# Reordering the first phase of a Fourier mixing and MLP kernel, with identity products in TensorE's waits

## The chip, the cores and the metric

The kernel runs on one core of a Trainium2 chip. The metric is the device time of one execution in microseconds (us). The median of eight runs of the kernel before is 1998.47 us (1996.56 to 2000.04).

The engines are named as in the profile: PE is TensorE's matrix product, PEld its weight load, DVE is VectorE, ACT is ScalarE, POOL is GpSimd and SP is SyncE, which here only issues transfers. The engines run side by side, and each takes its own instructions in the order in which the program issues them.

## What is computed

A real input of 8 x 3008 x 256 goes through a two-dimensional Fourier transform of which the real part is kept, and its rows then through an MLP with squared ReLU:

```python
def _attn_ref(x) -> np.ndarray:          # x: (8, 3008, 256)
    X = np.fft.fft(x, axis=1)
    X = np.fft.fft(X, axis=2)
    return X.real.astype(np.float32)

def _moe_ref(x, w_in, w_out) -> np.ndarray:   # w_in: (256, 2048), w_out: (2048, 256)
    h = x @ w_in
    r = np.maximum(h, 0.0)
    g = r * r
    return (g @ w_out).astype(np.float32)
```

The weights come as 64-bit floating point numbers and are converted to 32 bits on the chip. All products are in 32 bits; in the profile each one is two instructions.

## The kernel before

**Staging.** The transform along the 256 columns is not done on the data: it is multiplied into `w_in`, which gives the tables `G1`, `G2` and `gE`. The transform along the 3008 rows of a batch is a product of folded rows with tables of cosines and sines, and gives `Pt`, `Qt` and `Et` (the cosine part, the sine part, and one single column). The main loop then goes over 8 batches, 6 blocks of at most 251 frequencies and NJ = 8 parts of the 2048 hidden columns, 384 steps in all.

**One step of the loop.** `front` (L402) makes four products, for each of two halves one of `G1` with `Pt` (L412) and one of `G2` with `Qt` (L413), into PSUM tiles `ph`, and VectorE joins them with `Et` and `gE` into `g` (L415, L417, L418). `combine` (L425) lets ScalarE take ReLU and square (L427, L428). `back` (L443) multiplies `g` with `wout` two steps later (LAG = 2), into the PSUM tiles mA to mD. In the first block of the first batch (steps 0 to 7) it uses a plain form (L452) that needs only mA and mB; later steps use the form of L465. During batch b the rows of batch b + 1 are folded and transformed between the pieces of `front`.

**The first phase.** The first batch has nothing to hide behind. SP issues the loads of the first weight, the seven tiles of x and the cosine and sine tables, in this order. Then the following pieces are issued, in an order written out by hand (L568 to L595):

- `for_p(t)`: the three VectorE pieces of the fold that make `wP` of tile t (L297, L307, L308, L317). `for_q(t)`: the three that make `wQ` (L301, L312, L323). P and E are made of all seven `wP`, Q of all seven `wQ`.
- thirty groups, five for each of six transforms: P (0 to 4 and 5 to 9, even and odd frequencies), E (10 to 14, 15 to 19), Q (20 to 24, 25 to 29). In each five, the first is `even_n` (four products on TensorE from tiles 0 to 3, and a copy `da` by ScalarE, L357), the second and third are `join_4` and `join_2` (VectorE), the fourth is `odd_n` (three products from tiles 4 to 6), and the fifth `join_1` writes the result (L362 and L364 or L366). All products are at L349. Their PSUM tiles are two buffers, `psd`.
- the weights, in the order win 0, win 1, wout 0, win 2, wout 1, win 3 and so on. To begin one (`convert`, L187) issues its loads on SP, two VectorE passes (L208, L213) and three ScalarE passes (L210, L211, L215). Its `finish` is three VectorE passes (L218, L220, L221). For a `win` there are also its `products` (L232): `G1` and `G2` (two products each, L236, copied by ScalarE at L237) and `gE` (L242, L244). `next_weight` (L546) begins the next weight and then finishes the current one. The raw data has four buffers: three are shared with the tiles of x (tiles 4 to 6), one is a buffer of its own.

**Order within the loop.** In step i the program issues `front` and `combine`, then `back` of step i - 2, then the `products` collected by the step before, and then up to two calls of `next_weight`.

The clock of TensorE in the profile (PEclk) is the share that the throttle granted; 1.00 is full speed. Before its first change in a trace it is shown as 1.00; durations tell more there.

Of the kernel before, what the change touches and what calls it, by code (L numbers as in the profile page):

```python
# [8 lines left out]
F32 = mybir.dt.float32  # L9
# [4 lines left out]
P = 128  # L14
# [63 lines left out]
def kernel(  # L78
# [12 lines left out]
    nc = tc.nc  # L91
    B, NROW, _, D = x.shape
# [6 lines left out]
    NJ = NFC // 2  # L99
    CH = 256  # L100
# [22 lines left out]
    psm = ctx.enter_context(tc.tile_pool(name="psm", bufs=1, space=PSUM))  # L123
# [7 lines left out]
    def load_x(b, t):  # L131
        _, r0, step, rows = TILES[t]

        while rows % 15 and rows % 16 and r0 + step * rows < NROW:
            rows += 1

        pool, tag = (gp, "g") if b == 0 and t < NT - NX else (xp, "x")
        xt[b, t] = pool.tile([P, 4, D], F32, name="xt", tag=tag)
        nc.sync.dma_start(out=xt[b, t][0:rows], in_=x[b, r0:r0 + step * (rows - 1) + 1:step])
# [8 lines left out]
    ident = const.tile([P, P], F32, name="ident")  # L148
# [4 lines left out]
    def load_table(tab, src, engine):  # L153

        for t, (c, r0, step, rows) in enumerate(TILES):
            for i, (s0, count) in enumerate(row_tiles(S)):
                mine = [r for r in range(count) if (s0 + r - r0) % step == 0 and 0 <= (s0 + r - r0) // step < rows]
                if mine:
                    o, m = (s0 + mine[0] - r0) // step, len(mine)
                    while m % 15 and m % 16 and o + m < P and mine[0] + step * m < P:  # L160
                        m += 1
                    nk = NC[0][c]
                    engine.dma_start(out=tab[o:o + m, :, PLACE[t]:PLACE[t] + nk],
                                     in_=src[mine[0]:mine[0] + step * (m - 1) + 1:step, :, i, 0:nk])
# [4 lines left out]
    nc.vector.memset(ramp[:, 1:2], 255.0 * 2.0 ** 23)  # L169
    for dst, src in ((cosd, cos_d), (sind, sin_d), (altd, alt_d)):  # L170
        nc.scalar.dma_start(out=dst, in_=src.rearrange("(c p) m -> p c m", p=P))


    def pair_in(j):
# [77 lines left out]
    def sum_wout(j):  # L252

        b11, b12, b21, b22 = (wout[:, j, h, c] for c in range(2) for h in range(2))
        t2, t3, t4 = (wsum[:, i, j] for i in range(3))
        tt(out=t3, in0=b22, in1=b12, op=ALU.subtract)
        tt(out=b12, in0=b12, in1=b11, op=ALU.subtract)
        tt(out=t2, in0=b22, in1=b12, op=ALU.subtract)
        tt(out=t4, in0=t2, in1=b21, op=ALU.subtract)
# [9 lines left out]
    def load_column(t):  # L269

        _, r0, step, rows = TILES[t]
        xe[t] = const.tile([P, 4, NE], F32, name=f"xe{t}")
        for i in range(4):
            nc.sync.dma_start(out=xe[t][0:rows, i], in_=x[1:B, r0:r0 + step * (rows - 1) + 1:step, i, H].rearrange("b r -> r b"))
# [127 lines left out]
    def front(b, k0, n, j, between):  # L402

        pt, qt, et = PQE[b]
        ks = slice(k0, k0 + n)
        g = gp.tile([P, 2, 2, CK], F32, name="g", tag="g")
        for h in range(2):
            fc = j + NJ * h
            fs = slice(fc * P, (fc + 1) * P)
            ps = psh.tile([P, 2, CH], F32, name="ph", tag="h")  # L410
            hP, hQ = ps[:, 0, 0:n], ps[:, 1, 0:n]
            nc.tensor.matmul(hP, G1[:, fs], pt[:, ks], start=True, stop=True)  # L412
            nc.tensor.matmul(hQ, G2[:, fs], qt[:, ks], start=True, stop=True)  # L413
            t = hp.tile([P, CK], F32, name="he", tag="he")[:, 0:n]
            nc.vector.scalar_tensor_tensor(out=t, in0=et[:, ks], scalar=gE[:, fc:fc + 1], in1=hP,  # L415
                                           op0=ALU.mult, op1=ALU.add)
            tt(out=g[:, h, 0, 0:n], in0=t, in1=hQ, op=ALU.add)  # L417
            tt(out=g[:, h, 1, 0:n][:, ::-1], in0=t, in1=hQ, op=ALU.subtract)  # L418
            between()
        return g  # L420
# [17 lines left out]
        gt(out=s4, in0=g12, in1=s2, op=ALU.subtract)  # L438
        return s

    acc = {}

    def back(n, j, g, s, final):  # L443

        if j == 0:
            for nm in ("mA", "mB", "mC", "mD"):
                acc[nm] = psm.tile([P, 2, CH], F32, name=nm, tag=nm)
        if s is None:
            for c in range(2):
                for h in range(2):  # L450
                    for side, nm in enumerate(("mA", "mB")):
                        nc.tensor.matmul(acc[nm][:, h, 0:n], wout[:, j, h, c], g[:, c, side, 0:n],  # L452
                                         start=j == c == h == 0, stop=j == NJ - 1 and c == 1, skip_group_check=True)
            return
        products = [("mA", 0, wout[:, j, 0, 0], g[:, 0, 0]),
                    ("mA", 1, wout[:, j, 0, 1], g[:, 1, 0]),
                    ("mB", 0, wsum[:, 2, j], g[:, 1, 1]),
                    ("mB", 1, wout[:, j, 1, 0], s[:, 0]),
                    ("mC", 0, wsum[:, 0, j], s[:, 1]),
                    ("mC", 1, wsum[:, 1, j], s[:, 2]),  # L460
                    ("mD", 0, wout[:, j, 1, 1], s[:, 3])]
        if final and j == NJ - 1:
            products = products[0:2] + products[4:7] + products[2:4]
        for nm, i, w, v in products:
            nc.tensor.matmul(acc[nm][:, i, 0:n], w, v[:, 0:n], start=j == 0 and i == 0, stop=j == NJ - 1,  # L465
                             skip_group_check=True)
# [66 lines left out]
    def ahead(b):  # L533
        ops = [piece for t in range(NT) for piece in fold(b, t)] + dft_ops(b)
        if b == 1:
            ops += [(0.6, lambda t=t: fold_column(t)) for t in range(NT)] + dft_ops(None)
        return ops + [(0.0, lambda: load_e(b))] if b else ops
# [8 lines left out]
    def next_weight():  # L546

        nonlocal begun
        (finish, products), begun = begun, weights.pop(0)() if weights else None
        finish()  # L550
        return products
# [4 lines left out]
    def for_p(t):  # L556
        for i in (0, 2, 4):
            pieces[t][i]()

    def for_q(t):  # L560
        for i in (1, 3, 5):
            pieces[t][i]()

    def groups_at(*which):
        for i in which:
            groups[i]()

    begun = weights.pop(0)()  # L568
    for t in range(NT):
# [1 line left out]
    load_table(cosT, cos_s, nc.sync)  # L571
    load_table(sinT, sin_s, nc.sync)
    start()
    for_p(0)
    finish, products = begun
    finish()
    products()
    for t in range(1, 4):
        for_p(t)
    groups_at(0, 5)  # L580
    for_p(4)
    groups_at(1, 2)
    for_p(5)
    groups_at(6, 7)
    for_p(6)
    groups_at(3)
    for n, t in enumerate((4, 5, 6, 0, 1, 2, 3)):
        for_q(t)
        groups_at(*((4, 8, 9), (10,), (11, 12), (13, 14, 15), (16, 17), (18,), (19,))[n])
    groups_at(20, 25)  # L590
    begun = weights.pop(0)()
    groups_at(21, 22, 23)
    products = next_weight()
    groups_at(26, 27, 28, 24, 29)
    products = [products]  # L595
    LAG = 2
    BLOCKS = [(k0, min(CK, NKT - k0)) for k0 in range(0, NKT, CK)]
    steps = [(b, k0, n, j) for b in range(B) for k0, n in BLOCKS for j in range(NJ)]
# [15 lines left out]
    for i in range(len(steps) + LAG + 4):  # L614
        if i < len(steps):
            b, k0, n, j = steps[i]
            if i == NJ:
                for t in range(NX):
                    load_x(1, t)
            if NJ <= i < NJ + NT:  # L620
                load_column(i - NJ)
            if i % per == 0:
                assert not side
                side = ahead(b + 1) if b + 1 < B else []
                spent, pace = 0.0, sum(t for t, _ in side) / (2 * (per - (0 if i else 2 * NJ)) - 6)
            g = front(b, k0, n, j, between)
            if i < NJ:
                s = combine(n, g, True)
            elif i < 2 * NJ:
                sum_wout(j)  # L630
        while finished and finished[0][0] <= i:
            store(*finished.pop(0)[1:])
        if i >= LAG and flight:
            at, g_, s_ = flight.pop(0)
            final = at[:3] == (B - 1, *BLOCKS[-1])
            back(at[2], at[3], g_, s_, final)
            if at[3] == NJ - 1:
                c_ = gather(at[2], s_ is None, final)
                finished += [(i + 2 + s, *at[:3], s, c_, final) for s in range(2)]
        for f in products:  # L640
            f()
        products = [next_weight() for _ in range(2 if i + 2 < NJ else 1 if i < NJ else 0)]
        if i < len(steps):
            flight.append(((b, k0, n, j), g, s if i < NJ else combine(n, g, False)))

# [62 lines left out]
```

## Time and profile before

| | |
|---|---|
| median of 8 runs | 1998.47 us |
| profiled execution | 1999.46 us |
| its span | 1997.7 us |
| mean granted TensorE clock | 0.993 |
| busy PE / PEld | 1964.2 (98%) / 1706.0 (85%) us |
| busy DVE / ACT / POOL | 1390.6 (70%) / 896.4 (45%) / 1159.0 (58%) us |
| first product of `win` 0 on TensorE | 12.24 us |
| first product of `front`, step 0 | 54.93 us |
| first product of `front`, step 8, after which no weight is left to convert | 120.42 us |

The span runs from the first to the last recorded instruction of the one profiled execution; some 1.8 us of the execution lie around it. Busy time is the sum over the recorded instructions of an engine. A busy TensorE is not TensorE at its peak, since the records of products overlap and become longer where the clock is at half. In the timelines, a bracket at the end of a line gives the idle time of the engine just ahead of the instruction and who ended it.

### The profile page before, as it was taken

What the parts mean: (1) busy time and instruction counts of PE and PEld (TensorE: products, weight loads), DVE (VectorE), ACT (ScalarE), POOL (GpSimd) and SP (SyncE); (2) the same over time, 40 slices, a digit from 0 to 9 for tenths busy, and PEclk for the clock granted to TensorE, in tenths of its full rate; (3) what the DMA queues carried; (4) which work ended last, traced back from release to release, by engine and by line L of the source; (5) the groups of instructions that cost most, each with busy time, mean ns of one, the idle gap of its engine ahead of it and who ended that gap; (6) DMA issues with size and microseconds to landing.
All of it is one profiled execution on the core that took longest, in us unless ns stands there. A gap on an engine that the chain in (4) does not pass through costs nothing.

```text
span 1997.7 us, 27284 instructions
## 1 busy us (share of the span) xinstructions
PE 1964.2 (98%) x9104; PEld 1706.0 (85%) x9104; DVE 1390.6 (70%) x3492; ACT 896.4 (45%) x973; POOL 1159.0 (58%) x1695
## 2 busy tenths in 40 slices
PE   6899999999999999999999999999999999999998
PEld 4788888888888888888888888888888888888887
DVE  7889866776567765787558875677657776555554
ACT  1654434444444444444444444444444454445443
POOL 0026655666566755676556665666656665566664
PEclk8899999999999999999999999999999999999999
DMA  6332101210021111111011110111001100100100
GB/s 183 102 52 49 37 11 32 52 27 22 11 52 32 27 28 30 27 39 40 11 27 37 39 30 11 31 43 37 22 11 45 39 11 16 31 11 11 22 11 21
DMA packets 144687, 68.49 MB, mean 34 GB/s; under 512 B 128440, under 2 KB 135547, under 8 KB 144546
## 3 DMA queue, kind: packets, MB, share of 16 engines
q1 hardware_dynamic: 143470, 66.24, 14.3%
q8 instruction: 71, 1.16, 0.2%
q10 hardware_dynamic: 1076, 0.52, 0.1%
q14 instruction: 70, 0.57, 0.1%
HBM read 42.03 MB, written 24.68 MB: 33 GB/s over the span
## 4 chain that ended last, share of the span: by engine, by line
PE 94%; DVE 3%; ACT 1%; DMA 1%; issue 0%; SPq 0%; DVEq 0%; ACTq 0%
PE ph L412 16%; PE ph L413 16%; PE mA L465 16%; PE mC L465 16%; PE mB L465 16%; PE mD L465 8%; PE pd L349 5%; DMA xt<-in_x_dram 1%; DVE he L415 0%; PE mA L452 0%; PE mB L452 0%; DVE g L418 0%; PE pg L236 0%; DVE fd L301 0%; ACT g L427 0%
## 5 line engine op out<-in xcount | busy, mean ns | idle before, releaser
L427 ACT ACTIVATE g<-g 128x1004 f32<-128x1004 f32 (+1 forms) x384 | 399.5, 1040 | 895.4 <-DVE g L418 483.8
L415 DVE SCALAR_TENSOR_TENSOR he<-Et,gE,ph 128x251 f32<-128x251 f32 (+1 forms) x768 | 361.6, 471 | 476.1 <-PE ph L413 474.5
L435 POOL TENSOR_TENSOR s<-g 128x251 f32<-128x251 f32 (+1 forms) x376 | 248.6, 661 | 745.1 <-ACT g L428 672.3
L412 PE MATMUL ph<-Pt,G 128*128 128x251 f32 (+1 forms) x1536 | 454.3, 377 | 3.5 <-ACT G L237 2.5
L413 PE MATMUL ph<-Qt,G 127*128 127x251 f32 (+1 forms) x1536 | 452.2, 375 | 0.2 <-DVE Qt L362 0.2
L428 ACT ACTIVATE g<-g 128x1004 f32<-128x1004 f32 (+1 forms) x384 | 399.2, 1040 | 12.1
L465 PE MATMUL mC<-s,wsum 128*128 128x251 f32 (+1 forms) x1504 | 381.3, 374 | 0.0
L465 PE MATMUL mA<-g,wout 128*128 128x251 f32 (+1 forms) x1504 | 380.9, 375 | 0.0
L417 DVE TENSOR_TENSOR g<-he,ph 128x251 f32<-128x251 f32 (+1 forms) x768 | 320.4, 417 | 55.6 <-POOL s L437 0.5
L412 PEld LDWEIGHTS ph<-Pt,G 128*128 128x128 f32 x1536 | 287.7, 189 | 47.6 <-DVE g L418 4.0
L413 PEld LDWEIGHTS ph<-Qt,G 127*128 127x128 f32 x1536 | 291.7, 190 | 36.6 <-DVE Qt L362 0.6
L465 PEld LDWEIGHTS mA<-g,wout 128*128 128x128 f32 x1504 | 282.5, 189 | 41.7 <-issue 2.9
L465 PEld LDWEIGHTS mC<-s,wsum 128*128 128x128 f32 x1504 | 285.5, 190 | 34.5
L418 DVE TENSOR_TENSOR g<-he,ph 128x251 f32<-128x251 f32 (+1 forms) x768 | 314.0, 409 | 0.0
L436 POOL TENSOR_TENSOR s<-s,g 128x251 f32<-128x251 f32 (+1 forms) x376 | 281.7, 749 | 29.4
L437 POOL TENSOR_TENSOR s<-g 128x251 f32<-128x251 f32 (+1 forms) x376 | 291.8, 776 | 0.0
L438 POOL TENSOR_TENSOR s<-g,s 128x251 f32<-128x251 f32 (+1 forms) x376 | 246.2, 655 | 0.0
L465 PE MATMUL mB<-g,wsum 128*128 128x251 f32 (+1 forms) x752 | 220.4, 374 | 0.0
L465 PE MATMUL mD<-s,wout 128*128 128x251 f32 (+1 forms) x752 | 220.3, 374 | 0.0
L465 PE MATMUL mB<-s,wout 128*128 128x251 f32 (+1 forms) x752 | 219.9, 374 | 0.0
L465 PEld LDWEIGHTS mB<-g,wsum 128*128 128x128 f32 x752 | 142.6, 190 | 17.4
L465 PEld LDWEIGHTS mD<-s,wout 128*128 128x128 f32 x752 | 141.9, 189 | 17.7
(85 smaller groups left out, 1273.3 us busy)
## 6 DMA issues: line engine op xcount, KB each, us to landing
out_dram<-os SPq DMA_DIRECT2D x376, 56.0 KB
xt<-in_x_dram SPq DMA_DIRECT2D x24, 512.0 KB
xt<-in_x_dram SPq DMA_DIRECT2D x16, 384.0 KB
Et<-e_dram SPq DMA_DIRECT2D x7, 752.5 KB
out_dram<-os SPq DMA_DIRECT2D x288, 6.8 KB
raw<-in_moe_w_in_dram SPq DMA_DIRECT2D x16, 256.0 KB
raw<-in_moe_w_out_dram SPq DMA_DIRECT2D x16, 256.0 KB
xt<-in_x_dram SPq DMA_DIRECT2D x8, 480.0 KB
```

The costliest lines, as they stand in the source:

```text
L412: nc.tensor.matmul(hP, G1[:, fs], pt[:, ks], start=True, stop=True)
L413: nc.tensor.matmul(hQ, G2[:, fs], qt[:, ks], start=True, stop=True)
L415: nc.vector.scalar_tensor_tensor(out=t, in0=et[:, ks], scalar=gE[:, fc:fc + 1], in1=hP, op0=ALU.mult, op1=ALU.add)
L417: tt(out=g[:, h, 0, 0:n], in0=t, in1=hQ, op=ALU.add)
L418: tt(out=g[:, h, 1, 0:n][:, ::-1], in0=t, in1=hQ, op=ALU.subtract)
L427: act(v, v, AF.Relu)
L428: act(v, v, AF.Square)
L435: gt(out=s1, in0=g21, in1=g22, op=ALU.add)
L436: gt(out=s2, in0=s1, in1=g11, op=ALU.subtract)
L437: gt(out=s3, in0=g11, in1=g21, op=ALU.subtract)
L438: gt(out=s4, in0=g12, in1=s2, op=ALU.subtract)
L465: nc.tensor.matmul(acc[nm][:, i, 0:n], w, v[:, 0:n], start=j == 0 and i == 0, stop=j == NJ - 1, skip_group_check=True)
```

## The change

It has four parts, all of them in the first phase and the first steps of the loop.

1. A helper `awake(n)` issues n products of the identity with itself (128 x 128, 32 bits) into the second half of the PSUM tile mD, which the plain steps do not use. The tile is now allocated at the start and taken over by the first `back`.
2. `awake(24)` ahead of the first weight's products, `awake(8)` behind them, `awake(4)` behind each of the twelve `even_n` and `odd_n`, and `awake(8)` in step 1 of the loop, behind `front` and ahead of the products of win 2: 88 products in all.
3. The Q folds, which stood in one row behind the P transforms, are spread: those of tiles 0 and 1 stand ahead of the first `join_4`, those of 4, 5 and 6 between the P and E groups, those of 2 and 3 between the E groups.
4. Weights begin sooner. Win 1 begins behind group 13 instead of behind 25, and is finished (with wout 0 begun) ahead of group 21 instead of behind 23. A second `next_weight` (finish wout 0, begin win 2) stands ahead of groups 24 and 29; in return step 0 of the loop calls `next_weight` once instead of twice. From step 1 on, the loop issues the same weights in the same steps.

```diff
+    acc = {"mD": psm.tile([P, 2, CH], F32, name="mD", tag="mD")}
+    awoken = 0
+
+    def awake(n):
+
+        nonlocal awoken
+        for _ in range(n):
+            nc.tensor.matmul(acc["mD"][:, 1, 0:P], ident, ident, start=not awoken, stop=True, skip_group_check=True)
+            awoken += 1
...
-    acc = {}
-
     def back(n, j, g, s, final):
 
         if j == 0:
-            for nm in ("mA", "mB", "mC", "mD"):
+            for nm in ("mA", "mB", "mC") if len(acc) == 1 else ("mA", "mB", "mC", "mD"):
                 acc[nm] = psm.tile([P, 2, CH], F32, name=nm, tag=nm)
...
     def groups_at(*which):
         for i in which:
             groups[i]()
+            if i % 5 in (0, 3):
+                awake(4)
...
     start()
+    awake(24)
     for_p(0)
     finish, products = begun
     finish()
     products()
+    awake(8)
     for t in range(1, 4):
         for_p(t)
     groups_at(0, 5)
     for_p(4)
+    for_q(0)
+    for_q(1)
     groups_at(1, 2)
     for_p(5)
     groups_at(6, 7)
     for_p(6)
     groups_at(3)
-    for n, t in enumerate((4, 5, 6, 0, 1, 2, 3)):
-        for_q(t)
-        groups_at(*((4, 8, 9), (10,), (11, 12), (13, 14, 15), (16, 17), (18,), (19,))[n])
-    groups_at(20, 25)
+    for_q(4)
+    groups_at(4, 8)
+    for_q(5)
+    groups_at(9, 10)
+    for_q(6)
+    groups_at(11, 12, 13)
     begun = weights.pop(0)()
-    groups_at(21, 22, 23)
-    products = next_weight()
-    groups_at(26, 27, 28, 24, 29)
-    products = [products]
+    groups_at(15)
+    for_q(2)
+    groups_at(14, 16, 17, 18)
+    for_q(3)
+    groups_at(20, 19, 25)
+    products = [next_weight()]
+    groups_at(21, 22, 23, 26, 27, 28)
+    next_weight()
+    groups_at(24, 29)
...
+        if i == 1:
+            awake(8)
         for f in products:
             f()
-        products = [next_weight() for _ in range(2 if i + 2 < NJ else 1 if i < NJ else 0)]
+        products = [next_weight() for _ in range(2 if 0 < i < NJ - 2 else 1 if i < NJ else 0)]
```

## Prediction, made before the change was run

> **What bounds the kernel now.** I read the chain of waits first, then the page's 40 slices, then a table of stretches cut at the changes of TensorE's clock, then the timelines of VectorE and TensorE up to 130 us. The chain by engine:
>
> ```profile
> PE 94%; DVE 3%; ACT 1%; DMA 1%; issue 0%; SPq 0%; DVEq 0%; ACTq 0%
> ```
>
> The stretches (length, busy us and instructions of PE, PEld, DVE, ACT, POOL, then granted clock, DMA share, GB/s):
>
> ```profile
> 28.00:38.00 10.00, 7.86 (x30) 4.57 (x30) 9.50 (x27) 0.34 (x2) 0.00 (x0) 1.00 0.95 279
> 38.00:52.00 14.00, 13.20 (x28) 7.57 (x28) 11.46 (x33) 4.14 (x9) 0.00 (x0) 0.51 0.08 32
> 52.00:65.70 13.70, 9.11 (x38) 6.32 (x38) 10.98 (x25) 6.75 (x12) 0.00 (x0) 0.99 0.24 78
> 65.70:75.30 9.60, 9.04 (x25) 7.59 (x26) 7.08 (x16) 6.37 (x11) 0.00 (x0) 0.50 0.34 109
> 75.30:120.40 45.10, 43.13 (x216) 37.66 (x215) 38.88 (x84) 32.69 (x55) 0.00 (x0) 1.00 0.32 100
> 120.40:1997.70 1877.30, 1867.78 (x8733) 1632.78 (x8732) 1296.45 (x3264) 841.44 (x879) 1158.32 (x1689) 1.00 0.13 28
> ```
>
> The reader is to see two regimes. From 120.4 us to the end TensorE is busy in 1867.8 of 1877.3 us at full clock: nothing here is changed, and whatever the start gains or loses is carried to the end one for one. Before that no engine is full, and the clock is at half for 14 us and for 9.6 us. The change lies wholly before 75 us, so the question is how many us earlier the loop gets into its rhythm.
>
> In the loop's first eight steps the weights are converted, and step follows step as a ring: VectorE's `front` (2.33 us), ScalarE's two passes of `combine` (2.1), the copies to `G` and `gE` (0.6), ScalarE's three passes for the next `win` (2.1), VectorE's `finish` (1.95), `front` again. At full clock the ring takes 8.5 us (L208 of a step at 87.18, 95.68, 104.17). VectorE's waits on the way there, from its timeline (start, length, instruction, and in brackets the idle time before it):
>
> ```profile
> 22.69 0.25 DVE L362 TENSOR_TENSOR db<-da,pd 128x95 f32<-128x95 f32 x1 [3.37 <-ACT da L357]
> 49.81 0.69 DVE L218 SCALAR_TENSOR_TENSOR fd<-raw,fd 128x512 uint32<-128x512 uint32 x1 [2.23 <-ACT fd L211]
> 55.13 0.55 DVE L362 TENSOR_TENSOR Qt<-dc,pd 127x376 f32<-127x376 f32 x1 [1.40 <-PE pd L349]
> 63.02 0.69 DVE L218 SCALAR_TENSOR_TENSOR fd<-raw,fd 128x512 uint32<-128x512 uint32 x1 [0.75 <-ACT fd L211]
> 64.96 0.47 DVE L415 SCALAR_TENSOR_TENSOR he<-Et,gE,ph 128x251 f32<-128x251 f32 x1
> 73.15 0.69 DVE L218 SCALAR_TENSOR_TENSOR fd<-raw,fd 128x512 uint32<-128x512 uint32 x1 [2.38 <-ACT fd L211]
> 75.08 0.47 DVE L415 SCALAR_TENSOR_TENSOR he<-Et,gE,ph 128x251 f32<-128x251 f32 x1
> ```
>
> 64.96 is `front` of step 1, 75.08 of step 2; step 3 follows at 84.86, step 4 at 93.36. Steps 1 to 2 and 2 to 3 take 10.12 and 9.78 us, 2.9 us together over the rhythm of 8.5. TensorE's timeline shows why:
>
> ```profile
> 66.26 2.08 PE L236 MATMUL pg<-win,cosd 128*128 128x256 f32 x4 [2.96 <-DVE g L418]
> 78.64 1.02 PE L236 MATMUL pg<-win,cosd 128*128 128x256 f32 x4
> ```
>
> The same four products cost 2.08 us after the idle time and 1.02 later: the clock fell at 65.7, `gE` came late, and ScalarE's passes for `win` stand behind it.
>
> **The change, part by part.** *VectorE's order.* No instruction of it goes or comes before step 1's `front`; it is moved. Its waits from 19.3 to 64.96 us sum to 3.37 + 0.19 + 2.23 + 1.40 + 0.32 + 0.75 = 8.26 us. I lay the new order out with the old durations: a P fold 1.78, a Q fold 1.59, join_4 0.45, join_2 0.53, join_1 0.91, beginning a weight 0.67, finishing it 1.95, `front` 2.33. `for_q(0)` and `for_q(1)` (3.18) fill the 3.37 wait: join_4 stands at 22.5 instead of 22.69 with two Q folds done, and the last P fold ends at 28.04. From there TensorE's chain must be laid beside it.
>
> *TensorE.* An odd product takes 1.90 us at full clock (237.85 to 239.75), an even one 1.38 (231.69 to 233.07). The identity product is not in the trace. It has 128 columns; 251 columns take 0.2125 us an instruction and two instructions make a product, so 0.217 us; the nearest row of small products with full 128x128 loads, L242, goes at 0.10 us an instruction, so the load does not bind much lower. I take 0.22; at half clock 0.43. Four are 0.88, and the 88 make 19 us, of which those in true idle time cost nothing. The 24 at the start (10.3 us at half clock, from `ident` at 1.3 us to at most 11.7) end before `win` at 12.1; the next 8 lie in the wait for the cosine table, which lands at 18.5 and 20.5. From 28.04 on they cost: six odd, four even products and ten fours are 6 x 1.90 + 4 x 1.38 + 10 x 0.88 = 25.7 us, so `front` of step 0 can begin at 53.8 on TensorE. VectorE in its new order has 23.2 us of work there (five Q folds, six join_1, four pairs of joins, two weights begun and finished and one begun), so it waits here and there for TensorE: 0.4 before join_1 of P, 0.9 before join_4 of the second E group, 0.7 before the last join_1, 0.8 before `front`. TensorE, filled by useless products, is the one that is late next.
>
> *Weights earlier.* `win` 1 is begun at 36.3 instead of 45.2 and finished at 46.4; its raw data is issued behind the sine table as before (29.1). Summing the bytes landed by time, the table is in at 32.2 and that weight at 34.2, so 2 us to spare; were the slots shared, at 39.2 at the latest, 2.9 us of stall, of which about 2.3 would reach TensorE. `wout` 0 and the begin of `win` 2 (2.7 + 0.7 us) move ahead of the last two join_1, into time that VectorE waits in anyway. ScalarE takes `wout` 0's passes behind the second da copy of Q, at 47.6, and the finish needs them at 50. On SP the raw loads keep their order, and the next one comes free some 5 us sooner; the DMA share there is 0.08, so nothing collides. PSUM: each psd buffer is free before its product is due.
>
> *Step 0 and 1.* `front` 0 on VectorE at 54.7 (before 56.46), to 57.0; `combine` to 59.1, the `G` copies to 59.7, TensorE's `front` 1 at 59.45, VectorE's at 60.4, where begin and finish (2.6) are long done. The waits check this: the new ones sum to 4.1, and 64.96 - 8.26 + 4.1 = 60.8. Gain at step 1: 4.3 us. The eight products at step 1 end at 62.9, `win` 2's products could begin at 62.7, ScalarE is ready for them only at 64.8: 0.2 to 0.3 us lost.
>
> *The clock in steps 1 to 3.* The eight products stand where TensorE idled 2.96 us, and `win` 2 no longer waits for `wout` 0's finish. If the clock holds, the 2.9 us come back. Here a rule of the Trainium skill, "TensorE: Matmul & The Clock Gate", Part 1, speaks against this part: the clock falls only after an idle window of some 3.4 us, and rises after as long a busy one. By that rule a gap of 2.96 would do no harm and the eight products would bring nothing (gain 4.0). The trace differs: the clock was at half from 65.7, within that gap, and fell at 38.0 after gaps of 1.8 and 0.9 us; it rose only after 9.6 and 13.6 us of apparent work. I follow the rows: 4.3 + 2.9 - 0.3 = 6.9 us.
>
> *The clock at 28 us.* In the old trace the products at 28 us are slow until about 31. If that stays so, TensorE's chain loses 1.5 us and the sum is 5.4. With the fours between 21 and 27 us I hold full clock a little likelier. I take 6.5 us: the profiled execution goes from 1999.5 to 1993.0, and the median of the eight runs, 1998.5, to **1992.0**.
>
> **Rivals.**
>
> *TensorE's identity products eat the gain (1998).* The stretch from 38.0 to 51.65 shows 13.6 us at half clock with TensorE's records dense, so density alone did not raise it. Should such a stretch fall between 28 and 54 us, the 25.7 us chain loses 6.8 and the gain is 0.1. Against it: full-width products without gaps are denser than the small ones there. The gain is under 4 us as soon as the half-clock stretch passes some 6 us. Chance 0.24, with all ways in which less comes back (a late raw load, or the shift being swallowed by the 1.0 us of TensorE idle time between 200 and 240 us, which is too small to do it alone).
>
> *The slower side (2017).* The same place, the chain from 28 us, but the clock stays down all through it; that identity products count as work for the clock is shown by no row. Then 25.7 becomes 51.4 us: 25.7 lost against 6.9 gained, 18.8 net. It decides from a half-clock stretch of 22 us on (11 lost, 4 net). Against it: the old kernel never stayed down longer than 13.6 us once work was continuous. Chance 0.09.
>
> *More than forecast (1989.5).* If TensorE is never behind, VectorE's own work ends at 28.0 + 23.2 = 51.3, `front` 0 stands 2 us earlier than in my layout, and the gain is 9. It is in the first chance below.
>
> **How the numbers follow.** Faster by over 0.2% (4 us, about what a measurement of this kernel can tell from no change): my forecast and the case above, 0.67; within 4 us: 0.24; slower: 0.09. The range goes from the 9 us of the last case and a little run-to-run spread (1989.0) to the rival without gain (1998.5); about 2 in 10 lie outside.
>
> **What would show it.** Right: VectorE's `front` of step 1 at 60 to 61 us and of step 3 near 78 instead of 84.9; no clock of 0.5 between 55 and 76; the 3.37 and 2.23 waits gone; TensorE the releaser of VectorE's last Q joins. Wrong: products of 0.43 us between 30 and 54, the `front` of step 0 after 57, or steps 1 to 3 still at 10 us each.

## The result and the profile after

The changed kernel takes 1992.86 us (median of 11 runs, 1991.46 to 1994.67) beside 1998.64 us for the kernel before on the same chip: a ratio of 0.9971, 95% interval 0.9963 to 0.9978. The prediction was 1992.0, with 1989.0 to 1998.5 as its range. The profiled execution has a span of 1992.9 us (before 1997.7) and a mean clock of 0.996. It took 1994.67 us and is the slowest of the eleven; the profiled execution before (1999.46) is 0.8 us above its median. So times read from the two profiles differ by 4.8 us where the medians differ by 5.8.

The chain of waits of the changed kernel has hardly moved; the gain is too small a part of it to be seen there:

```profile
PE 95%; DVE 2%; ACT 1%; DMA 1%; issue 0%; SPq 0%; DVEq 0%
```

The stretches of the changed kernel (columns as before: length, PE, PEld, DVE, ACT, POOL, granted clock, DMA share, GB/s), cut where its clock changes:

```profile
21.00:31.00 10.00, 10.00 (x31) 7.51 (x32) 8.10 (x26) 0.48 (x2) 0.00 (x0) 0.50 0.71 196
31.00:57.00 26.00, 26.00 (x150) 19.97 (x149) 21.80 (x58) 6.81 (x13) 0.00 (x0) 1.00 0.48 148
57.00:76.00 19.00, 17.94 (x100) 15.34 (x98) 16.70 (x38) 13.13 (x21) 0.00 (x0) 1.00 0.27 84
```

The two stretches of half clock at 38 and 66 us are gone; what is left is one from 21 to 31. Only its last 3 us are new. Before, TensorE was at half clock up to 27.8 us, where the trace has its first change of the clock, as the products of the first two odd parts of P show:

```profile
25.02 2.88 PE L349 MATMUL pd<-cosT,wP 128*128 128x377 f32 x4
28.91 2.06 PE L349 MATMUL pd<-cosT,wP 128*128 128x376 f32 x6
```

Four instructions took 2.88 us at half clock, and six of almost the same width 2.06 us at full clock just behind them. From 31 to 57 us TensorE's records leave no gap at all, while VectorE is busy for 21.8 of 26 us: VectorE now waits for TensorE. Its timeline, changed kernel:

```profile
26.61 0.25 DVE L373 TENSOR_TENSOR db<-da,pd 128x94 f32<-128x94 f32 x1 [1.49 <-ACT da L368]
31.71 0.55 DVE L373 TENSOR_TENSOR Pt<-dc,pd 128x377 f32<-128x377 f32 x1 [0.66 <-PE pd L360]
42.12 0.26 DVE L373 TENSOR_TENSOR db<-da,pd 128x94 f32<-128x94 f32 x1 [0.87 <-ACT da L368]
55.15 0.55 DVE L373 TENSOR_TENSOR Qt<-dc,pd 127x376 f32<-127x376 f32 x1 [0.89 <-PE pd L360]
56.90 0.48 DVE L426 SCALAR_TENSOR_TENSOR he<-Et,gE,ph 128x251 f32<-128x251 f32 x1 [0.74 <-PE ph L424]
63.00 0.48 DVE L426 SCALAR_TENSOR_TENSOR he<-Et,gE,ph 128x251 f32<-128x251 f32 x1 [1.08 <-PE ph L424]
71.58 0.47 DVE L426 SCALAR_TENSOR_TENSOR he<-Et,gE,ph 128x251 f32<-128x251 f32 x1
80.08 0.47 DVE L426 SCALAR_TENSOR_TENSOR he<-Et,gE,ph 128x251 f32<-128x251 f32 x1
```

The waits of 3.37 and 2.23 us are gone, and smaller ones stand in their place, 6.2 us in all up to step 1, of which the six longest are shown. The last four lines are `front` of steps 0 to 3. Before, steps 0 and 3 stood at

```profile
56.46 0.48 DVE L415 SCALAR_TENSOR_TENSOR he<-Et,gE,ph 128x251 f32<-128x251 f32 x1 [0.32 <-PE ph L413]
84.86 0.47 DVE L415 SCALAR_TENSOR_TENSOR he<-Et,gE,ph 128x251 f32<-128x251 f32 x1
```

and steps 1 and 2 at 64.96 and 75.08. So `front` comes 0.4 us later in step 0, 2.0 earlier in step 1, 3.5 in step 2 and 4.8 in step 3. From there to the end of the span it is 1912.8 us in both kernels (1992.9 - 80.08 and 1997.7 - 84.86), and 1912.7 to 1912.9 in every kernel below. Whatever is won by step 3 is the whole effect.

TensorE in the changed kernel:

```profile
28.10 3.58 PE L360 MATMUL pd<-cosT,wP 128*128 128x377 f32 x6
31.51 1.06 PE L181 MATMUL mD<-ident 128*128 128x128 f32 x8
32.40 2.06 PE L360 MATMUL pd<-cosT,wP 128*128 128x376 f32 x6
55.84 0.59 PE L423 MATMUL ph<-Pt,G 128*128 128x251 f32 x2
```

The first odd product took 3.41 us to the next start, mostly at half clock; the second took 1.90. `front` of step 0 could begin at 55.84 only.

### The profile page after: what moved, and what is told of

Same layout as the page of the kernel before. It is cut to its first block, busy times and chain, and to the rows that moved or that the text cites. A ratio compares the mean times of both kernels' runs of the same rounds, so it can differ in the third digit from the quotient of the medians.

```text
span 1992.9 us, 27635 instructions
## 1 busy us (share of the span) xinstructions
PE 1973.5 (99%) x9280; PEld 1721.5 (86%) x9280; DVE 1390.6 (70%) x3492; ACT 896.2 (45%) x973; POOL 1158.7 (58%) x1695
## 4 chain that ended last, share of the span: by engine, by line
PE 95%; DVE 2%; ACT 1%; DMA 1%; issue 0%; SPq 0%; DVEq 0%
PE ph L423 16%; PE ph L424 16%; PE mA L474 16%; PE mC L474 16%; PE mB L474 16%; PE mD L474 8%; PE pd L360 6%; PE mD L181 1%; DMA xt<-in_x_dram 1%; DVE he L426 0%; DVE g L429 0%; ACT g L438 0%; ACT g L439 0%; DVE g L428 0%; PE mB L461 0%
```

## The experiments

The first fold of VectorE waits for x, and its start differs from execution to execution by up to 1.5 us (7.69 to 9.22 us in the profiles below); what follows on VectorE moves with it, where no wait takes that up. So the table counts `front` of steps 1 and 3 from the first fold. The medians are of 5 to 20 runs; before was 1998.2 to 1998.6 beside each of them.

| kernel | step 1 | step 3 | median us | ratio to before (95%) |
|---|---|---|---|---|
| before | 56.6 | 76.5 | 1998.6 | 1 |
| changed | 54.7 | 71.8 | 1992.86 | 0.9971 (0.9963 to 0.9978) |
| e1 order only | 51.5 | 68.5 | 1990.61 | 0.9961 (0.9948 to 0.9973) |
| e2 identity only | 56.7 | 73.7 | 1997.45 | 0.9995 (0.9987 to 1.0003) |
| e3 no fours | 52.6 | 69.7 | 1993.48 | 0.9973 (0.9964 to 0.9982) |
| e4 no eight in step 1 | 55.2 | 72.2 | 1992.87 | 0.9975 (0.9966 to 0.9985) |
| e6 folds only | 51.8 | 71.8 | 1994.12 | 0.9974 (0.9964 to 0.9983) |
| e7 weights only | 54.9 | 71.9 | 1995.33 | 0.9985 (0.9978 to 0.9991) |
| e8 eights for fours | 64.4 | 81.4 | 2002.12 | 1.0017 (1.001 to 1.0023) |
| e9 order and fours | 55.1 | 72.1 | 1994.78 | 0.998 (0.9971 to 0.9989) |
| e10 order only, again | 52.4 | 69.4 | 1992.65 | 0.9972 (0.9961 to 0.9983) |
| e11 changed, again | 53.0 | 70.1 | 1993.74 | 0.9977 (0.997 to 0.9985) |
| e12 order, two fours | 51.0 | 68.0 | 1991.27 | 0.9968 (0.9956 to 0.9981) |
| e5 targeted | 53.6 | 70.6 | 1991.6 | 0.9972 (0.9962 to 0.9982) |

The columns of the profile are of one execution each and agree with the medians to some 2 us: e11 and the changed kernel are the same program and differ by 1.7. Where the argument rests on less than that, the medians decide. The profiled executions of e4 and of the changed kernel are the slowest of their runs, and that of e12 is the fastest.

### The two halves of the change, each alone

e1 leaves out all 88 identity products:

```diff
-            if i % 5 in (0, 3):
-                awake(4)
...
-    awake(24)
...
-    awake(8)
...
-        if i == 1:
-            awake(8)
```

> The new order of VectorE's work and of the weights, without any identity product. My theory: the order gives most of the gain, the identity products give the clock but take TensorE's time back, so 3 to 5 us faster than before (1993.5 to 1995.5); the 3.37 and 2.23 us waits are gone from VectorE, front of step 1 near 61 to 63 us, and a stretch of half clock stays somewhere between 38 and 76 us. Rival 'it is all the clock': within 1 us of before (1998). Rival 'the identity products only cost': faster than the changed kernel, 1991 or less.

Measured: 1990.61 us, 7.8 below before. VectorE's waits in e1 up to step 1, and its stretch from 57 to 76 us:

```profile
32.34 0.55 DVE L373 TENSOR_TENSOR Pt<-dc,pd 128x376 f32<-128x376 f32 x1 [0.90 <-PE pd L360]
42.81 0.55 DVE L373 TENSOR_TENSOR Et<-dc,pd 128x376 f32<-128x376 f32 x1 [1.20 <-PE pd L360]
53.12 0.47 DVE L426 SCALAR_TENSOR_TENSOR he<-Et,gE,ph 128x251 f32<-128x251 f32 x1 [0.32 <-PE ph L424]
59.21 0.48 DVE L426 SCALAR_TENSOR_TENSOR he<-Et,gE,ph 128x251 f32<-128x251 f32 x1 [1.08 <-PE ph L424]
```

```profile
57.00:76.00 19.00, 16.94 (x85) 14.27 (x85) 16.07 (x34) 15.42 (x28) 0.00 (x0) 1.00 0.35 112
```

The order brings at least the whole gain, and the clock is full in steps 1 to 3 without any help. My 3 to 5 us were too few; the rival "only cost" named this number (1991 or less), but the repetition e10, further down, at 1992.65, does not reach it.

e2 has the old order and all identity products (the hand-written order and the calls of `next_weight` are those of before).

> The old order with all 88 identity products in the same places. My theory: they keep the clock up in steps 1 to 3, which is worth at most 2.9 us, and cost about as much where the fours stand ahead of useful products at half clock: 0 to 2 us faster than before (1996.5 to 1998.5), VectorE's waits of 3.4 and 2.2 us still there. Rival 'it is all the clock': 4 to 6 us faster (1992.5 to 1994.5). Rival 'the identity products only cost': 2 us or more slower than before (2000 or more).

Measured: 1997.45; the interval includes no change at all. In its profile the clock is full from 20 us on, and yet step 1 does not come earlier (56.7 against 56.6); steps 1 to 3 win the 2.8 us that were put down to the clock. That is one of the faster executions (1996.14); the median is only 0.9 us under before, so the other executions kept less of it, and why is not shown. The wait that the folds were to fill is there as it was:

```profile
21.92 0.25 DVE L373 TENSOR_TENSOR db<-da,pd 128x95 f32<-128x95 f32 x1 [3.11 <-ACT da L368]
```

### Which identity products do anything

e3 drops the two lines `if i % 5 in (0, 3): awake(4)`; e4 drops `if i == 1: awake(8)`.

> The changed kernel without the twelve fours behind the DFT products; 24, 8 and 8 stay. If the fours make TensorE the late one (VectorE waited 1.5, 0.7, 0.9 and 0.9 us for it), front of step 0 comes near 54 instead of 56.9 us and the time is 1 to 2.5 us under the changed kernel (1990.5 to 1992). If they are what holds the clock from 31 us on, the clock is at half for some 10 us between 31 and 60 and the time is 1 to 3 us above the changed kernel (1994 to 1996).

> The changed kernel without the eight products in step 1. They end at 65.4 us, where win 2's products could begin at 64.2. If the clock falls in gaps of 2 to 3 us only, the gap left is about 0.6 us, the clock holds, and the time is that of the changed kernel within 0.5 us (1992.5 to 1993), step 2 at 71.3 to 71.6 us. If they are what holds the clock in steps 1 to 3, half clock follows near 66 to 75 us and 2 to 3 us are lost (1995).

e3: `front` of step 0 came at 54.56 us, as the first reading said, and the clock fell, as the second said (half from 23.5 to 33.7 us and from 40.5 to 43.9). The median, 1993.48, lies between the times of the two readings. The runs show both effects: the five with a mean clock of 0.994 to 0.996 took 1991.0 to 1992.3 us, the six with 0.992 or 0.993 took 1993.5 to 1994.9.

e4: the same time as the changed kernel (1992.87), clock full from 31.4 us on. TensorE in e4, where the eight had stood:

```profile
63.91 0.59 PE L424 MATMUL ph<-Qt,G 127*128 127x251 f32 x2
65.06 1.13 PE L247 MATMUL pg<-win,cosd 128*128 128x256 f32 x4 [0.56 <-DVE g L429]
```

A gap of 0.56 us is all that they filled. What took the gap of 2.96 us out of step 1 is the order: `wout` 0 is no longer finished there (e7, below, shows it without identity products).

### The order taken apart

e6 keeps the new order of the folds and puts the weights back behind group 25; e7 keeps the old order of the folds and begins the weights as in the change. Neither has identity products.

```diff
     groups_at(11, 12, 13)
-    begun = weights.pop(0)()
...
     groups_at(20, 19, 25)
-    products = [next_weight()]
-    groups_at(21, 22, 23, 26, 27, 28)
-    next_weight()
-    groups_at(24, 29)
+    begun = weights.pop(0)()
+    groups_at(21, 22, 23)
+    products = next_weight()
+    groups_at(26, 27, 28, 24, 29)
+    products = [products]
```

> No identity products; the folds in the new order, the weights where they were before. New theory: the new order alone brings the 8 us that order-only showed, and the weights bring more of it than the folds. Then this one fills the 3.37 us wait, keeps the 2.2 us wait for win 1 and the fall of the clock in steps 1 to 2: 2 to 3.5 us faster than before (1995 to 1996.5). Rival 'the folds bring it': 5 us or more faster (1993.5 or less).

> No identity products; the weights begun and finished early as in the change, the Q folds in the old order. New theory: without wout 0's finish in step 0, win 2's products come in time, TensorE has no gap of 3 us there and the clock holds without identity products; 4.5 to 6 us faster than before (1992.5 to 1994), the 3.4 us wait for the first da still there, no half clock between 55 and 76 us. Rival 'the folds bring it': 3 us or less (1995.5 or more).

Measured: 4.0 us for the folds and 2.8 for the weights, so my split was the wrong way round: both times are outside what the theory expected, though the waits and the clock of e7 are as expected. The profiles tell why. With the folds alone, `front` of step 1 comes 4.8 us earlier and that of step 3 4.7: TensorE in e6 still has the old gap, and the clock falls behind it:

```profile
57.68 0.59 PE L424 MATMUL ph<-Qt,G 127*128 127x251 f32 x2
61.23 2.07 PE L247 MATMUL pg<-win,cosd 128*128 128x256 f32 x4 [2.96 <-DVE g L429]
```

With the weights alone step 1 comes 1.7 us earlier and step 3 4.6: the gap is down to 0.56 us, the clock holds, and the 2.9 us of steps 1 to 3 come back. TensorE in e7, and its stretch from 57 to 76 us:

```profile
65.07 1.13 PE L236 MATMUL pg<-win,cosd 128*128 128x256 f32 x4 [0.56 <-DVE g L418]
```

```profile
57.00:76.00 19.00, 16.90 (x82) 13.62 (x82) 16.51 (x38) 12.33 (x21) 0.00 (x0) 1.00 0.26 83
```

Together (e1) it is 5.1 at step 1 and 8.0 at step 3. So the folds win the time ahead of step 1, and the weights that of the clock. The profiles put it at some 5 and 3 us; the sizes hold only to some 2 us, since at step 3 the two alone are 4.7 and 4.6 us earlier, and in the medians they are worth 4.0 and 2.8. In the profile of e2 the identity products win the same 3 us; where the weights are early they have nothing left to win there.

### What the fours cost

```diff
             if i % 5 in (0, 3):
-                awake(4)
+                awake(8)
```

> The changed kernel with eight products instead of four behind each DFT product. If TensorE is the late one from 28 us on, ten times four more products of 0.22 us put front of step 0 later by 8 to 9 us (near 65.5 instead of 56.9) and the time to 1999 to 2002. If VectorE hides them, the time stays within 1 us of the changed kernel.

> The new order with the twelve fours alone (no 24, no 8, no 8). If the fours cost (they delay TensorE's useful products) the time is 2 to 4 us above order-only (1992.5 to 1994.5), front of step 0 near 57 instead of 53.1 us. If the 24 and the first 8 are what costs, it is that of order-only within 0.7 us (1990.6).

e8: 9.3 us above the changed kernel (2002.12 - 1992.86), `front` of step 0 at 66.52 instead of 56.90. TensorE and VectorE of e8 just ahead of it:

```profile
61.78 2.06 PE L360 MATMUL pd<-sinT,wQ 128*127 128x376 f32 x6
63.69 1.95 PE L181 MATMUL mD<-ident 128*128 128x128 f32 x16
65.47 0.59 PE L423 MATMUL ph<-Pt,G 128*128 128x251 f32 x2
```

```profile
63.89 0.55 DVE L373 TENSOR_TENSOR Qt<-dc,pd 127x376 f32<-127x376 f32 x1 [2.68 <-PE pd L360]
66.52 0.48 DVE L426 SCALAR_TENSOR_TENSOR he<-Et,gE,ph 128x251 f32<-128x251 f32 x1 [1.63 <-PE ph L424]
```

Forty-eight more products cost 9.6 us at step 0, 0.20 us each; one takes 0.22 (eight in the 1.78 us from 63.69 to 65.47). So hardly any of them is hidden. e9, the order with the fours alone, has the step 1 of the changed kernel (55.1, 54.7) and not that of e1 (51.5); its median is 4.2 above e1 and 2.1 above e10. Without the 24 and the eights, VectorE's waits in e9 are those of the changed kernel (1.54, 0.45, 0.87, 0.89, 0.74, 1.08 us).

### Are the identity products a net cost, and is there a better place

e10 and e11 repeat e1 and the changed kernel on one chip. e12 is e1 with four products behind groups 10 and 15 (`if i in (10, 15): awake(4)`). e5 has 24 at the start, 20 behind the first weight's products, 16 behind group 5, four behind groups 10 and 15, and none in step 1.

> The order-only kernel once more, on the same chip as the changed kernel. If the identity products are a net cost it stays 1.5 to 3 us under the changed kernel (ratio to before near 0.996). If the difference of the first series came from the few runs, both agree within 0.7 us.

> The changed kernel once more, beside order-only. Expected 5 to 6 us under before (ratio near 0.997), front of step 0 near 57 us.

> Order-only with four identity products behind the two even products of E and nowhere else. In order-only TensorE waits 1.6 us there, the clock falls at 39 us, and VectorE then waits 1.2 us for the last product of E. If the fours hold the clock there, that wait goes and the time is 0.5 to 1.2 us under order-only. If they only delay, it is 0 to 1 us above.

> The new order with 24 products at the start, 20 behind the first weight's products, 16 behind the second even product of P, 4 behind each even product of E, none elsewhere: the identity products put where TensorE has nothing to do. If holding the clock from the start is worth something, VectorE's waits of 0.9 and 1.2 us in order-only go and the time is 1 to 2 us under it. If the clock falls in the first 20 us all the same, the 20 run at half clock, end after 21 us, delay the first even product, and the time is 1 to 3 us above order-only.

On one chip the order alone is 1.1 us under the changed kernel, less than the 1.5 to 3 expected. Over all runs of the two (12 and 25, in two series each) the means differ by 1.8 us, give or take 0.9. The identity products bring nothing in the new order, and probably cost 1 to 3 us. e12 has the lowest median of its series and the earliest step 3 of all profiles (of its fastest run), and the 1.2 us wait of e1 is not in it; but with five runs its interval covers that of e10. That e12 beats e1 is not shown; that both are at least as good as the change is.

e5 went the second way at first: TensorE, and VectorE's wait behind it,

```profile
1.36 7.13 PE L181 MATMUL mD<-ident 128*128 128x128 f32 x48 [1.36 <-POOL ident masks.py:199]
12.60 2.08 PE L247 MATMUL pg<-win,cosd 128*128 128x256 f32 x4 [4.11 <-DVE win L232]
17.74 6.55 PE L181 MATMUL mD<-ident 128*128 128x128 f32 x40
24.12 2.92 PE L360 MATMUL pd<-cosT,wP 95*128 95x95 f32 x16
```

```profile
25.88 0.25 DVE L373 TENSOR_TENSOR db<-da,pd 128x95 f32<-128x95 f32 x1 [3.04 <-ACT da L368]
```

The 24 raised the clock (they end at 8.5 us, where half clock would take until 11.7), it fell in the 4.1 us of waiting for the first weight, and the 20 ran for 6.4 us, mostly at half clock, in front of the first even product. In return VectorE has only 0.2 us of waits from there until 54 us. This execution, at 1993.89 us, is one of three near 1994; the five others took 1990.6 to 1991.7, and no profile shows whether they lost as much at the start. The median of 1991.6 is between those of e12 and e10: a better place than none is not shown.

## Why the prediction was right, point by point

- **The whole before 75 us, carried to the end one for one**: right, to 0.1 us (1912.8 us from step 3 to the end, before and after).
- **VectorE's new order**: right up to its last P fold, which ended at 29.4 instead of 28.0 us; the 1.4 us are the wait for the second da (1.49 us), which I had not seen: four identity products at half clock stood in front of the second even product. Without the fours (e3) this wait is absent, and where the clock was still full for the first of them (e11) it is 0.29 us.
- **TensorE as the late one from 28 us on**: right, and e8 shows it. Its size was off: I had 25.7 us from the first odd product to `front` of step 0, and it took 27.7 (28.10 to 55.84). 1.5 of it is the first product at half clock, which the prediction had kept as its other case (its ground for it was misread, see below); 0.5 is the fours, 0.89 us behind an odd product and 1.00 behind an even one, against 0.88.
- **Step 1 at 60.4**: it came at 63.0, a gain of 2.0 instead of 4.3. This is the term that was mis-sized: 2.0 of the 2.6 us come from TensorE's chain, 0.4 from steps 0 to 1 (6.1 instead of 5.7 us). Of the signs named for "right", step 1 at 60 to 61 us is missed, step 3 near 78 too (80.1; in the repetition 61.7 and 78.8), and `front` of step 0 at 56.9 almost meets the sign of "wrong", after 57.
- **2.9 us of the clock in steps 1 to 3**: 2.8 came back. Of the two reasons given with it, the early `wout` 0 is the one (e1, e4, e7); the eight products filled 0.56 us.
- **The rule of the Trainium skill against the rows**: the choice for the rows held. "TensorE: Matmul & The Clock Gate", Part 1, has the clock fall only behind an idle window of some 3.4 us. In e6 it fell again within a gap of 2.96 us, and no kernel without that gap shows a fall there. When it fell, TensorE had been idle for 2.25 us (58.27 to 60.52), and in the kernel before for 2.05 (63.30 to 65.35), less than the page's window. The earlier fall, at 38.04 us, came 0.2 us into the second of the two gaps that the prediction names, not after it.
- **The clock at 28 us** was held a little likelier to be full. In the changed kernel it was at half from 21 to 31 us, in its repetition from 22.5 to 29.3. And the old trace was misread: its products were not slow until 31 us, since from 28.2 us on they ran at full clock (the two lines at 25.02 and 28.91 above). That the other case came about is not what the old trace showed.
- **The rival on the slower side** did not come: once TensorE had no gaps, the clock rose within 10 us. e8 shows that its price was real: what is added to TensorE's chain (9.6 us at step 0) reaches the end (9.3 us in the median).
- **Waits for the raw weights**: 2 us to spare was too good, though in the changed kernel nothing waits for them; e10 shows 0.89 us of waiting for `win` 1.

The median came out 0.9 us above the forecast, and that it is so near is in part luck: in the profiles 4.8 of the 6.9 us of the sum came, and the repetition of the same program (e11) gained 4.4. What the prediction left out is the order without identity products. Its own sum has 8.8 us of fours in TensorE's chain, and its last case, TensorE never behind and `front` of step 0 two us earlier, is nearly what the order alone did (53.1 us in e1). The order is worth 7.8 us in e1 and 5.5 in e10, and the identity products take some of it back.

## What to carry to other kernels

Work that only keeps TensorE busy is paid almost in full (here 0.20 us a product) wherever another engine waits for what TensorE does behind it; count TensorE's chain with the filler in it, at half clock too, before adding any. Where the clock falls in a gap, look for the gap's cause first: here the weights begun earlier, so that one conversion leaves step 0, brought it from 2.96 to 0.56 us without any of the 88 products (e7). And where two parts of a change are aimed at the same loss, time each alone, since the second one may only cost.

## What the runs showed of the hardware that was not expected

- Density of records does not tell whether the clock rises. In the changed kernel TensorE's records leave no gap from 21.8 to 28 us (3.7 us of identity products, 2.5 of an even product with 94 to 188 columns), and the clock stayed at half until 31. The 24 identity products at the start, without gaps, took 7.1 to 8.6 us in the seven profiles that have them, less than the 10.3 us of half clock.
- The clock changes only on a grid. In each of the 14 profiles all its changes lie whole multiples of 3.41 us apart; before they are at 27.80, 38.04, 51.69, 65.35 and 75.59 us, which is 3, 4, 4 and 3 of them. So the same gap can lie differently to the grid from one execution to the next. How full TensorE's records are between two grid points does not settle it either: 40% ahead of the fall at 65.35 us, but 43% from 45.57 to 48.98 in e1, where the clock stayed, and 79% from 20.06 to 23.47 in e3, where it fell.
- The same program differs in when its first data lands (e1 and e10: the first fold at 7.69 and 9.22 us), and by several us in where its clock falls (e1: at 38.7 us, e10: at 41.8 and 48.6). From step 3 to the end all 14 profiles take 1912.7 to 1912.9 us, so these differences lie ahead of step 3.
